# Branch prefetch notes, earlier flag reads and per-pair sink values in a fused attention and mixture-of-experts kernel

## The chip, the cores and the metric

The kernel runs on one core of a Trainium2 chip. The metric is the device time of one execution in microseconds; the time of before is the median of three runs. TensorE (PE, with its weight loads as PEld) multiplies, VectorE (DVE) and ScalarE (ACT) work on its results, GpSimd (POOL) does some elementwise work and the indirect DMAs, and SyncE (SP) issues the other DMAs. Each engine has a sequencer that runs its own program in order: it issues instructions to the engine, waits for semaphores, reads registers from memory and branches.

## The reference

Three stages follow each other, all in float32:

```python
scores = scale * np.matmul(q, k.transpose(0, 1, 3, 2))     # 2 batches, 8 heads, 768 positions, head size 64
keep = is_sink | in_window                                 # first 4 keys, and a window of 128
a = softmax(np.where(keep, scores, -1e9));  attn = a @ v   # reshaped to x: 1536 x 512
for e in range(4):                                         # first mixture: every token, every expert
    out += p[:, e:e + 1] * (np.maximum(x @ w1[e], 0.0) @ w2[e])
idx = argmax(normalised x @ normalised expert_emb / tau)   # second mixture: one of 8 experts per token
out[idx == e] = gate * (np.maximum(x[idx == e] @ w1[e], 0.0) @ w2[e])
```

How many tokens each of the eight experts of the second mixture gets depends on the data.

## The kernel before

Matrix products run as three products of rounded halves (a high part and the remainder), so each float32 operand is first split by a cast (the high part) and a subtraction (the low part).

**Attention** (`Attention.narrow_path`) works on eight pairs of heads. Its instructions are put in order by a small planner (`Order`), which knows for each operation the engine, a planned cost, the operations that it comes after and a rank; it simulates the engines' times and, for each engine, issues among the operations that could start first the one of lowest rank. Loads are operations of SP in this plan. For a query block, scores are made on TensorE (line 365), masked on VectorE (378), put through the exponential on ACT into a probability buffer P (384; two buffers, used by pairs in turn), normalised on POOL (403), transposed on TensorE (410, 412), copied (415) and multiplied with the values (449). The weights of the sink keys are gathered apart and multiplied with the sinks' values in `vsr` (440). `vsr` holds the sinks' values of all eight pairs; it is zeroed at the start by VectorE and POOL and filled by eight DMAs in `vsload` (313). The kernel is written for narrow windows; after attention a flag decides whether a general path recomputes it (`tc.If(att.narrow < 1)`, line 1388). With these inputs it is skipped. `Moe1.first` runs the first hidden layer ahead of that branch, and the first mixture follows it.

**The first mixture** (`moe1`) is a long straight run of matmuls (lines 980 and 1035) with no branch in it.

**The second mixture** (`Moe2.run`) gathers the tokens of an expert in slots of 128 rows. An expert has one slot at least and up to twelve; how many is known only at run time. So each further slot stands in an If inside the one before (`more_slots`): if the flag `over` for slot k + 1 is 0, the program jumps past all the rest of this expert's slots to the next expert. The flag is read from memory into a register of every engine by `Route.has` (line 966, `values_load`); `announced` calls it and marks a branch-hint location. Before, that call names no engines. The bodies are the fall-through side, so the jump is the way out. On the way out each engine runs a few semaphore catch-ups, which wait for its own work so far and raise the counts that the skipped slots would have raised. In the trace they and the branches have line 1297, those of the general path line 1388.

Within a slot (`slot`) the matmuls come in 16 named places: a0 to a3 and b0 to b3 for the first layer, t0 and t1 for transposes of the hidden rows, c0 to c7 for the second layer. Hooks put other engines' work behind these places: the splitting of the next expert's weights (`Fill`, lines 668, 670 and 674) on ACT, VectorE and POOL, with the load of a later chunk behind each, the transposes of the next slot's tokens (1070), and the scaling and scattering of the slot before (1116, 1117). In the first slot of an expert and in the slots inside the Ifs, the flag of the next slot is read ahead of the slot's first matmul:

```python
c = announced(e, 1)
s.gather(xg[1], e, 1)
...
s.paced(e, 0, x0, w, Fill(its, busy), {"c2": [s.split_tokens(xg[1], x1)], ...})
more_slots(e, w, range(1, NT), c)
```

Only expert 0, whose second slot always runs, reads its flag inside a slot, behind place b3.

Of the kernel before, what the change touches and what calls it, by code (L numbers as in the profile page):

```python
# [19 lines left out]
P = 128  # L20
B, H, S, HD = 2, 8, 768, 64
NH = B * H
# [15 lines left out]
SPLIT3 = ((0, 0), (0, 1), (1, 0))  # L38
RANK = dict(
    sc=-1.86, mask=-1.68, exp=2.32, recip=1.03, norm=5.82, scp=-0.61, spe=2.96, sev=1.51, pt=2.75, ev=6.07, av=6.4, avs=4.76, xhi=11.43,  # L40
    xlo=1.57, qpe=-6.05, qhi=-8.82, qlo=-11.56, kpe=-4.73, khi=-2.69, klo=1.91, qld=-11.4, kld=-11.4, vld=-7.72, wld=0, Lpt=5.73, Lsc=-2.22,
    Lav=8.22, Lexp=-2.63, Lnorm=3.72, Lkpe=-4.67, Lavs=11.14, Lrecip=2.17, Lxlo=5.65, Lkhi=-5.14, Lxhi=9.92, Lev=6.37, Lscp=-0.42,
    Lsev=1.82,
)
SLACK = dict(PE=0.02, ACT=0.17, DVE=0.06, POOL=0, SP=0)
GROUP = ((0, 1), (1, 2), (2, 3), (3, 4), (4, 5), (5, 6))
LASTG = ((0, 2), (2, 4), (4, 6))
IOTA = dict(allow_small_or_imprecise_dtypes=True)


# [153 lines left out]
class Attention:  # L204


    def __init__(s, tc, st, c0, ps, q, k, v, n_sink, window, x, ident):

        s.tc, s.nc = tc, tc.nc
        s.q, s.k, s.v, s.x, s.ident = q, k, v, x, ident  # L210
        nc = s.nc
        c1 = st.enter_context(tc.tile_pool(name="a1", bufs=1))
        s.qk = [[c1.tile([P, 6, 2, HD], F32, name=f"{n}r{i}") for i in range(2)] for n in "qk"]
        s.vt = [c1.tile([P, 6, 2, HD], F32, name=f"vt{n}") for n in range(3)]
        s.qs = [c1.tile([P, 2, S], F32R, name=f"qs{n}") for n in range(2)]
        s.kk = [c1.tile([P, 2, 2, KW // 2], F32R, name=f"kk{n}") for n in range(2)]
        s.ksr = c1.tile([NS, NH, HD], F32, name="ksr")
        s.vsr = c1.tile([P, NH // 2, 4, P], F32, name="vsr")
        s.pp = ps.tile([P, 2, 512], F32, name="prep")
        s.xo = [ps.tile([P, 512], F32, name=f"xo{a}") for a in range(2)]  # L220
        V, A, G = nc.vector, nc.scalar, nc.gpsimd
        s.dum = c1.tile([P, P], BF16, name="dum")
        V.memset(s.dum, 0.0)
        s.busy(s.xo[1], 26)
        words = c0.tile([P, 2, 2], I32, name="words")
        h0, h1 = slice(0, 3), slice(3, 6)
        s.load(0, 0, h0)
        s.load(0, 1, h0)
        for i, src in enumerate((n_sink, window)):
            nc.sync.dma_start(out=words[:, i], in_=src.bitcast(I32).partition_broadcast(P))  # L230
        nc.sync.dma_start(out=s.ksr, in_=k[:, :, 0:NS, :].rearrange("b h s d -> s (b h) d"))
        s.load(0, 0, h1)
        s.load(0, 1, h1)
        s.load(1, 0)
        s.load(1, 1)
        s.vload(0)
        e = c1.tile([1, 1], F32, name="warm")
        V.memset(e, 0.0)
        A.activation(e, e, AF.Exp)
        s.rel = c1.tile([P, 2 * P], F32, name="rel")  # L240
        s.key = c1.tile([P, P], F32, name="key")
        G.iota(s.rel, pattern=[[-1, 2 * P]], base=P, channel_multiplier=1, **IOTA)
        G.iota(s.key, pattern=[[1, P]], base=0, channel_multiplier=0, **IOTA)
        G.affine_select(
            out=s.rel, in_=s.rel, pattern=[[-1, 2 * P]], compare_op=ALU.is_ge, fill=3.0e38, base=P, channel_multiplier=1
        )
        s.sk = [c1.tile([P, 4, 32], F32, name=f"sk{n}") for n in range(2)]
        s.masks = c1.tile([P, 4, W], F32, name="masks")
        for t in s.sk:
            G.memset(t, 0.0)  # L250
        V.memset(s.vsr[:, :4], 0.0)
        G.memset(s.vsr[:, 4:], 0.0)
        G.memset(s.masks[:, 0, P:], -1.0e30)
        G.memset(s.masks[:, 1, 2 * P :], -1.0e30)
        s.q_pe(0, s.pp[:, 0], 0)
        s.busy(s.xo[1], 6)
        s.k_pe(0, s.xo[0], 0)
        s.busy(s.xo[1], 18)
        s.q_hi(0, s.pp[:, 0], 0)
        s.k_hi(0, s.xo[0], 0)  # L260
        s.q_lo(0, s.pp[:, 0], 0)
        nw = int64_as_float(nc, c0, words, 2)
        s.nsf, s.wf = nsf, wf = nw[:, 0:1], nw[:, 1:2]
        fl = c1.tile([1, 2], F32, name="fl")
        fi = c1.tile([1, 1], I32, name="fi")
        V.tensor_scalar(fl[:, 0:1], nsf[0:1], float(NS), None, ALU.is_le)
        V.tensor_scalar(fl[:, 1:2], wf[0:1], -1.0, 128.0, ALU.mult, ALU.add)
        V.scalar_tensor_tensor(fl[:, 1:2], wf[0:1], -1.0, fl[:, 1:2], ALU.add, ALU.mult)
        V.scalar_tensor_tensor(fi, fl[:, 1:2], 0.0, fl[:, 0:1], ALU.is_ge, ALU.mult)
        s.k_lo(0, s.xo[0], 0)  # L270
        s.make_masks(c1)
        s.vsload()
        s.narrow = nc.values_load(fi[0:1, 0:1], min_val=0, max_val=1)

    def busy(s, t, n):
# [29 lines left out]
        for x in range(2):  # L305
            s.nc.sync.dma_start(out=s.vt[g % 3][:, :, x, :], in_=s.v[b, h0 + x].rearrange("(c p) d -> p c d", p=P))

    def vsload(s):

        for r in range(4):  # L310
            for x in range(2):
                o = 32 * r + NS * x
                s.nc.sync.dma_start(
                    out=s.vsr[o : o + NS, :, r, x * HD : (x + 1) * HD], in_=s.v[:, x::2, 0:NS, :].rearrange("b h s d -> s (b h) d")
                )

    def q_pe(s, g, pp, a):
        for c in range(3):
# [25 lines left out]
    def narrow_path(s, ctx, late, parts):  # L344
# [5 lines left out]
        masks, sk = s.masks, s.sk  # L350
        skT = [c1.tile([P, P], F32, name=f"skT{n}") for n in range(2)]
        V, A, G = nc.vector, nc.scalar, nc.gpsimd
        hp_ = ctx.enter_context(tc.tile_pool(name="ahd", bufs=2))
        sm = ctx.enter_context(tc.tile_pool(name="asm", bufs=4))
        ps1 = ctx.enter_context(tc.tile_pool(name="aps1", bufs=2, space=PSUM))
        xh, xl = s.x[:, 0], s.x[:, 1]
# [80 lines left out]
        def av_sink(g, i):  # L437
            o = (i % 3) * P
            xo = pr[g]["xo"]
            nc.tensor.matmul(xo[i // 3][:, o : o + P], vsr[:, g, i - 2], skT[g % 2], start=False, stop=True, skip_group_check=True)  # L440

        def av(g, c):
            px, xo = pr[g]["ptx", c], pr[g]["xo"]
# [34 lines left out]
        def all_(name, g, i=range(6), par=(0,)):  # L478
            return [(name, g, x, y) for x in i for y in par]
# [3 lines left out]
        for g in range(NP):  # L483
            groups = LASTG if g == NP - 1 else GROUP
            add("qld", g, 0, 0, dict(SP=2.2 if g else 0.0), lambda e, g=g: g > 1 and s.load(g, 0), [("qpe", g - 2, 0, 0)])
            add("kld", g, 0, 0, dict(SP=2.2 if g else 1.0), lambda e, g=g: g > 1 and s.load(g, 1), [("kpe", g - 2, 0, 0)])
            add("vld", g, 0, 0, dict(SP=2.2 if g else 5.0), lambda e, g=g: g and s.vload(g), all_("av", g - 3) + ([] if g else [("kld", 1, 0, 0)]))
            old = all_("sc", g - 2, par=AB)
            if not g:
                add("qpe", 0, 0, 0, dict(PE=0.32), lambda e: s.q_pe(0, pp[:, 1], 1), [("qld", 0, 0, 0)])  # L490
# [43 lines left out]
                    old.append(("klo", g, 0, 0) if g == NP - 1 else ("xlo", g - 1, c // 2, 0))  # L534
                add("av", *k, dict(PE=0.47 if c < 5 else 0.24), lambda e, g=g, c=c: av(g, c), old)
            for i in range(2, 6):
                add("avs", g, i, 0, dict(PE=0.215), lambda e, g=g, i=i: av_sink(g, i), [("sev", g, 0, 0), ("av", g, i, 0)])
            for a in AB:
                old = all_("avs", g, range(3, 6) if a else [2]) + [("av", g, 3 * a + 2, 0)]
                add("xhi", g, a, 0, dict(ACT=0.37), lambda e, g=g, a=a: x_hi(g, a), old)  # L540
# [561 lines left out]
class Moe2:  # L1102
# [159 lines left out]
    def run(s, psT, sp, wts, hx, wAB):  # L1262
# [26 lines left out]
        def announced(e, k):  # L1289

            c = R.has(e, k)
            tc.mark_branch_hint_location(f"more{e}_{k}", c)
            return c

        def more_slots(e, w, ks, first):

            with ExitStack() as nest:  # L1297
                c = first
                for k in ks:
                    nest.enter_context(tc.If(c > 0, label=f"more{e}_{k}", preferred_fallthrough_block=True))  # L1300
                    more = {}
                    if k < ks[-1]:
                        c = announced(e, k + 1)
                        s.gather(xg[1], e, k + 1)
                        more["c2"] = [s.split_tokens(xg[1], x1)]
                    s.paced(e, k, x1, w, Fill([], busy), more)

        for e in range(E2):
# [3 lines left out]
            if e == 0:  # L1312
                s.gather(xg[0], 1, 0)
                s.gather(xg[1], 0, 2)
                g = s.late
                n = []
                s.second(
                    w,
                    s.x1,
                    Fill(its, busy),  # L1320
                    {
                        "start": g[1:2],
                        "a1": g[2:3],
                        "a3": g[3:4],
                        "b3": g[4:5] + [lambda: n.append(announced(0, 2))],
                        "c2": g[5:] + [s.split_tokens(xg[0], x0)],
                        "c4": [s.split_tokens(xg[1], x1)],
                    },
                )
                more_slots(0, w, range(2, NT), n[0])  # L1330
            else:
                c = announced(e, 1)
                s.gather(xg[1], e, 1)
                if nxt:
                    s.gather(xg[0], e + 1, 0)
                s.paced(e, 0, x0, w, Fill(its, busy), {"c2": [s.split_tokens(xg[1], x1)], "c4": [s.split_tokens(xg[0], x0)] if nxt else []})
                more_slots(e, w, range(1, NT), c)
        s.flush()

    def split_tokens(s, t, o):  # L1340
# [6 lines left out]
def fused(tc, q, k, v, n_sink, window, probs, w1, w2, emb, tau, w1b, w2b, out):  # L1347
# [6 lines left out]
    with st:  # L1354
# [12 lines left out]
        with ExitStack() as sG:  # L1367
# [15 lines left out]
            hx = pool(st, "hx", 2, reuse_waits="tile")  # L1383
            psa = pool(st, "psa", 2, space=PSUM, reuse_waits="tile")
            m1 = Moe1(nc, wts, x, wA, hp, hx, psa)
            tc.mark_branch_hint_location("general", "LikelyTaken")
            m1.first()
            with tc.If(att.narrow < 1, label="general", preferred_fallthrough_block=True):  # L1388
                with ExitStack() as sN:
# [76 lines left out]
```

## Time and profile before

| | us |
|---|---|
| runs: lowest, median, highest of 3 | 914.21, 915.52, 917.66 |
| profiled execution | 916.67 |
| its span, first to last instruction | 914.9 |
| TensorE busy | 875.0 (96%) |
| VectorE busy | 426.8 (47%) |
| ScalarE busy | 303.7 (33%) |
| GpSimd busy | 189.7 (21%) |

The span is the time between the first and the last instruction on the core; the execution's time has a little around it. A timeline row gives start, length, engine, line, operation, tile, shape and how many instructions were merged; brackets at its end give the idle time of the engine before it and what ended that. A q behind an engine (PEq) is its sequencer. Matmul ends are modelled. Reads of registers, branches and semaphore instructions are not counted as busy; the views by line list them with their own lengths, as shortest/median/longest in nanoseconds and the first and last start.

### The profile page before, as it was taken

What the parts mean: (1) busy time and instruction counts of PE and PEld (TensorE: products, weight loads), DVE (VectorE), ACT (ScalarE), POOL (GpSimd) and SP (SyncE); (2) the same over time, 40 slices, a digit from 0 to 9 for tenths busy, and PEclk for the clock granted to TensorE, in tenths of its full rate; (3) what the DMA queues carried; (4) which work ended last, traced back from release to release, by engine and by line L of the source; (5) the groups of instructions that cost most, each with busy time, mean ns of one, the idle gap of its engine ahead of it and who ended that gap; (6) DMA issues with size and microseconds to landing.
All of it is one profiled execution on the core that took longest, in us unless ns stands there. A gap on an engine that the chain in (4) does not pass through costs nothing. (4 is left out here: it accounts for less than half of the span.)

```text
span 914.9 us, 11858 instructions
## 1 busy us (share of the span) xinstructions
PE 875.0 (96%) x4274; PEld 684.3 (75%) x4274; DVE 426.8 (47%) x1013; ACT 303.7 (33%) x664; POOL 189.7 (21%) x284
## 2 busy tenths in 40 slices
PE   8999998999999999999999999999998898898997
PEld 6766666878888888888888888888886676676775
DVE  5786854121234121233121235868547959717611
ACT  4777852020303010302010312111334646525422
POOL 4576510010000000000000000030405737516411
PEclk9999999999999999999999999999999999999999
DMA  7566200030032000023000013000445858727100
GB/s 137 92 144 149 66 24 5 1 116 1 0 93 91 3 0 1 1 92 92 1 1 1 4 66 104 35 12 34 130 154 172 260 156 276 256 74 220 63 34 23
DMA packets 84147, 72.83 MB, mean 80 GB/s; under 512 B 43572, under 2 KB 68148, under 8 KB 84040
## 3 DMA queue, kind: packets, MB, share of 16 engines
q1 hardware_dynamic: 81000, 65.25, 25.0%
q0 software_dynamic: 3040, 6.30, 2.0%
q8 instruction: 49, 0.80, 0.4%
q14 instruction: 58, 0.48, 0.2%
HBM read 68.10 MB, written 7.09 MB: 82 GB/s over the span
## 5 line engine op out<-in xcount | busy, mean ns | idle before, releaser
L1035 PE MATMUL po<-wA,h 128*128 128x512 f32 x1152 | 275.1, 398 | 4.0 <-DVEq L1388 4.0
L980 PE MATMUL ph<-x,wA 128*128 128x512 f32 x1152 | 271.8, 395 | 0.0
L1035 PEld LDWEIGHTS po<-wA,h 128*128 128x128 f32 x1152 | 216.1, 189 | 56.4 <-ACTq L1388 4.4
L980 PEld LDWEIGHTS ph<-x,wA 128*128 128x128 f32 x1152 | 215.2, 187 | 52.7
L982 ACT ACTIVATE h<-ph 128x512 fp32r<-128x512 f32 x96 | 57.4, 597 | 392.4 <-PE ph L980 390.7
L983 DVE SCALAR_TENSOR_TENSOR h<-ph,h 128x512 fp32r<-128x512 f32 x96 | 66.4, 692 | 173.0 <-ACT h L982 173.0
L57 POOL TENSOR_TENSOR gn<-gn,rss 128x4 f32<-128x4 f32 x9 | 1.8, 198 | 443.3 <-DVE gn L55 442.8
L674 DVE TENSOR_TENSOR wA<-raw,wA 128x512 fp32r<-128x512 f32 x107 | 81.3, 789 | 7.2 <-ACT wA L668 5.7
L1045 DVE SCALAR_TENSOR_TENSOR acc<-po,pr,acc 128x512 f32<-128x512 f32 x36 | 27.0, 750 | 110.0 <-PE po L1035 110.0
L668 ACT CAST wA<-raw 128x512 fp32r<-128x512 f32 x115 | 65.9, 618 | 6.4 <-PEq L1297 5.7
L403 POOL TENSOR_TENSOR P<-P,r 128x264 f32<-128x264 f32 (+1 forms) x87 | 54.1, 647 | 48.8 <-DVE r L397 19.5
L1172 PE MATMUL po<-wA,ht 128*128 128x512 f32 x216 | 57.7, 404 | 2.4 <-DVE ht L1166 2.3
L1166 DVE TENSOR_TENSOR ht<-hT,ht 128x512 fp32r<-128x512 f32 x30 | 20.6, 688 | 66.7 <-ACT ht L1165 63.8
L384 ACT ACTIVATE P<-m,nm 128x264 f32<-128x264 f32 x96 | 49.0, 512 | 8.3 <-DVE nm L378 7.9
L1149 PE MATMUL ph<-wA,xt 128*128 128x512 f32 x168 | 43.7, 410 | 7.4 <-PEq L966 7.4
L1172 PEld LDWEIGHTS po<-wA,ht 128*128 128x128 f32 x216 | 38.9, 188 | 11.4 <-DVE ht L1166 3.6
L378 DVE CUSTOM_DVE_ANT_0 m<-sc,masks 128x264 f32<-128x264 f32 x96 | 38.8, 429 | 16.6 <-PE sc L365 15.0
L1149 PEld LDWEIGHTS ph<-wA,xt 128*128 128x128 f32 x168 | 31.9, 194 | 15.7 <-ACTq L1297 6.9
L1149 PE MATMUL ph<-wB,xt 128*128 128x512 f32 x144 | 36.3, 401 | 7.1 <-PEq L966 7.1
L1172 PE MATMUL po<-wB,ht 128*128 128x512 f32 x144 | 39.3, 407 | 3.5 <-DVE ht L1166 3.5
L365 PE MATMUL sc<-kk,qs 64*128 64x264 f32 x288 | 41.6, 339 | 0.7 <-DVE nm L378 0.5
L674 DVE TENSOR_TENSOR wB<-raw,wB 128x512 fp32r<-128x512 f32 x44 | 37.5, 882 | 6.3 <-ACT wB L668 6.1
(222 smaller groups left out, 868.2 us busy)
## 6 DMA issues: line engine op xcount, KB each, us to landing
raw<-in_moe_w_dram SPq DMA_DIRECT2D x96, 512.0 KB
vt<-in_v_dram SPq DMA_DIRECT2D x16, 192.0 KB
xs<-acc SPq DMA_DIRECT2D x12, 256.0 KB
qr<-in_q_dram SPq DMA_DIRECT2D x14, 192.0 KB
kr<-in_k_dram SPq DMA_DIRECT2D x14, 192.0 KB
raw<-en SPq DMA_DIRECT2D x4, 512.0 KB
qr<-in_q_dram SPq DMA_DIRECT2D x4, 96.0 KB
kr<-in_k_dram SPq DMA_DIRECT2D x4, 96.0 KB
```

What stands on the lines that cost most here:

```text
L365: nc.tensor.matmul(sc[:, :W], qs[z, x, i * P : (i + 1) * P], kk[z, y, START[i] : START[i] + W], start=(n == 0), stop=(n == 2))
L378: V.tensor_tensor_reduce(m, t["sc", par][:, :W], masks[:, VAR[i]], -1.0, 3.0e38, ALU.add, ALU.min, t["nm"][:, par, i : i + 1])
L384: A.activation(t["P"][:, par, i], t["m", par, i], AF.Exp, scale=-1.0, bias=t["nm"][:, par, i : i + 1], accum_out=t["su"][:, par, i : i + 1],)
L403: eng.tensor_tensor(y, y, t["r", a][:, par].unsqueeze(2).to_broadcast([P, b - a, W]), ALU.mult)
L668: eng.copy(dst()[:, 0], r)
L674: eng.tensor_tensor(d[:, 1], r, d[:, 0], ALU.subtract)
L980: nc.tensor.matmul(ph, s.wA.w1(a, k, f * P)[:, :P], s.x[:, b, k, tb * TB : (tb + 1) * TB], start=(n == 0), stop=(n == 11))
L982: nc.scalar.activation(t[:, 0], ph, AF.Relu)
L983: nc.vector.scalar_tensor_tensor(t[:, 1], ph, 0.0, t[:, 0], ALU.max, ALU.subtract)
L1035: nc.tensor.matmul(po, hs[f][:, a, t * P : (t + 1) * P], wA.w2(b, f), start=(n == 0), stop=(n == 23))
L1149: nc.tensor.matmul(ph[b], x[:, a, kk], w.w1(c, kk, b * 512), start=(kk == 0 and n == 0), stop=(kk == 3 and n == 2),)
L1172: nc.tensor.matmul(s.po[0], ht[b][:, a, c * P : (c + 1) * P], w.w2(d, f), start=(f == 0 and n == 0), stop=(f == 7 and n == 2),)
```

## The change

Four edits:

- The two calls that mark branch hints name all five engines (`HINTED`), so that each gets a prefetch note: for the general path a fixed one (likely taken), for a slot's flag one that goes by the register.
- The flag of the next slot is read behind place a2 of a slot, and not ahead of its first matmul. The gathers that came behind the read now come ahead of it.
- `vsr` is two buffers of one pair each, used in turn. `vsload(g)` loads one pair by eight DMAs; pair 0's come at the start, the others are an operation `vsl` of SP in the plan, with a rank and a planned cost of 0.8, after the sink matmuls of two pairs before. A pair's sink matmuls come after it. POOL zeroes both buffers.
- P has three buffers. The planner's rule for the exponentials stays as it was.

```diff
+    ... vld=-7.72, vsl=-4, wld=0, ...
+ET = mybir.EngineType
+HINTED = (ET.PE, ET.Activation, ET.DVE, ET.Pool, ET.SP)
...
-        s.vsr = c1.tile([P, NH // 2, 4, P], F32, name="vsr")
+        s.vsr = [c1.tile([P, 4, P], F32, name=f"vsr{n}") for n in range(2)]
...
-        V.memset(s.vsr[:, :4], 0.0)
-        G.memset(s.vsr[:, 4:], 0.0)
+        for t in s.vsr:
+            G.memset(t, 0.0)
...
-    def vsload(s):
-
+    def vsload(s, g):
+
+        b, h0 = divmod(g * 2, H)
         for r in range(4):
             for x in range(2):
                 o = 32 * r + NS * x
-                s.nc.sync.dma_start(
-                    out=s.vsr[o : o + NS, :, r, x * HD : (x + 1) * HD], in_=s.v[:, x::2, 0:NS, :].rearrange("b h s d -> s (b h) d")
-                )
+                s.nc.sync.dma_start(out=s.vsr[g % 2][o : o + NS, r, x * HD : (x + 1) * HD], in_=s.v[b, h0 + x, 0:NS])
...
-        hp_ = ctx.enter_context(tc.tile_pool(name="ahd", bufs=2))
+        hp_ = ctx.enter_context(tc.tile_pool(name="ahd", bufs=3))
...
+            if g:
+                add("vsl", g, 0, 0, dict(SP=0.8), lambda e, g=g: s.vsload(g), all_("avs", g - 2, range(2, 6)))
...
-                add("avs", ..., [("sev", g, 0, 0), ("av", g, i, 0)])
+                add("avs", ..., [("sev", g, 0, 0), ("av", g, i, 0), ("vsl", g, 0, 0)])
...
-            tc.mark_branch_hint_location(f"more{e}_{k}", c)
+            tc.mark_branch_hint_location(f"more{e}_{k}", c, engines=HINTED)
...
                     if k < ks[-1]:
-                        c = announced(e, k + 1)
+                        more["a2"] = [lambda: c.append(announced(e, k + 1))]
                         s.gather(xg[1], e, k + 1)
...
-                c = announced(e, 1)
+                n = []
                 s.gather(xg[1], e, 1)
...
-                s.paced(e, 0, x0, w, Fill(its, busy), {"c2": ...})
-                more_slots(e, w, range(1, NT), c)
+                s.paced(e, 0, x0, w, Fill(its, busy), {"a2": [lambda: n.append(announced(e, 1))], "c2": ...})
+                more_slots(e, w, range(1, NT), n[0])
...
-            tc.mark_branch_hint_location("general", "LikelyTaken")
+            tc.mark_branch_hint_location("general", "LikelyTaken", engines=HINTED)
```

## Rows read from the trace of the kernel before

**Rows 1.** The page's busy times: engine, us, share of the span, instructions.
```profile
PE 875.0 (96%) x4274; PEld 684.3 (75%) x4274; DVE 426.8 (47%) x1013; ACT 303.7 (33%) x664; POOL 189.7 (21%) x284
```
**Rows 2.** Stages: us, length; busy PE, PEld, DVE, ACT, POOL; clock, DMA share, GB/s.
```profile
28.00:124.00 96.00, 95.42 (x751) 65.56 (x747) 74.82 (x292) 75.11 (x223) 57.64 (x101) 1.00 0.44 96
124.00:156.00 32.00, 27.48 (x138) 21.35 (x136) 14.66 (x25) 13.03 (x25) 0.00 (x0) 1.00 0.06 19
156.00:681.00 525.00, 524.82 (x2302) 421.16 (x2303) 184.94 (x410) 93.49 (x176) 22.50 (x61) 1.00 0.14 44
716.00:909.00 193.00, 172.68 (x804) 133.87 (x804) 109.59 (x163) 88.97 (x163) 80.20 (x62) 0.99 0.47 152
```
**Rows 3.** TensorE's waits, whole span: us in total, times, longest.
```profile
PE ph L1149 <- PEq L966: 14.5, 7, 3.1
PE po L1172 <- DVE ht L1166: 5.8, 7, 1.2
PE po L1035 <- DVEq L1388: 4.0, 1, 4.0
```
**Rows 4.** Timeline of TensorE and its weight loads in the second mixture.
```profile
758.53 2.35 PE L1172 MATMUL po<-wA,ht 128*128 128x512 f32 x9
...
762.81 3.32 PEld L1149 LDWEIGHTS ph<-wB,xt 128*128 128x128 f32 x15 [2.38 <-issue]
...
780.68 5.28 PE L1149 MATMUL ph<-wA,xt 128*128 128x512 f32 x15 [3.08 <-PEq L966]
...
809.08 3.67 PE L1149 MATMUL ph<-wA,xt 128*128 128x512 f32 x15
```
**Rows 5.** TensorE's sequencer on lines 1297 and 966: all, and around 760 us.
```profile
L1297 PEldq COMPARE_BRANCH  x18: 65/193/5233, 711.6 to 909.0; - x18
...
L1297 PEldq EVENT_SEMAPHORE  x2: 51/51/51, 762.2 to 762.3; - x2
L1297 PEldq COMPARE_BRANCH  x1: 4119/4119/4119, 758.0 to 758.0; - x1
...
L966 PEldq TENSOR_LOAD <-tr x14: 299/302/322, 707.6 to 892.6; - x14
```
**Rows 6.** The join of the general path: sequencers of line 1388, and timeline.
```profile
L1388 PEldq EVENT_SEMAPHORE  x1: 51/51/51, 152.0 to 152.0; - x1
...
L1388 DVEq EVENT_SEMAPHORE  x1: 21/21/21, 155.8 to 155.8; - x1
...
152.58 0.69 DVE L983 SCALAR_TENSOR_TENSOR h<-ph,h 128x512 fp32r<-128x512 f32 x1 [2.10 <-ACT h L982]
...
155.93 1.40 PE L1035 MATMUL po<-wA,h 128*128 128x512 f32 x5 [4.01 <-DVEq L1388]
```
**Rows 7.** As rows 2, two microseconds behind one change of expert.
```profile
782.00:784.00 2.00, 2.00 (x6) 1.61 (x5) 2.00 (x2) 0.00 (x0) 1.97 (x2) 0.50 0.89 299
```
**Rows 8.** Timeline: VectorE around that change; TensorE and ACT at the end.
```profile
778.75 1.88 DVE L674 TENSOR_TENSOR wA<-raw,wA 128x512 fp32r<-128x512 f32 x3
...
782.49 1.96 DVE L670 CAST wB<-raw 128x512 fp32r<-128x512 f32 x1
...
904.59 3.74 PE L1172 MATMUL po<-wB,ht 128*128 128x512 f32 x15
...
908.86 0.69 ACT L1116 ACTIVATE os<-po,curg 128x512 f32<-128x512 f32 x1 [3.35 <-PEq L1297]
```
**Rows 9.** Attention: the sinks' DMAs on SP, and waits of SP, ACT, PEld.
```profile
L313 SPq DMA_DIRECT2D vsr<-in_v_dram x8: 272/302/964, 11.1 to 15.2; - x8
...
SPq L306 <- PE xo L449: 50.8, 5, 14.5
...
ACT P L384 <- DVE nm L378: 7.9, 22, 0.8
...
PEld pt L410 <- issue: 5.3, 17, 0.4
```
**Rows 10.** Queue of TensorE's instructions, 156 to 681 us: packets, MB, share.
```profile
q8 instruction: 18, 0.29, 0.2%
```

More of the change, by code (lines that the diff above doesn't have):

```diff
@@ L40 @@
     sc=-1.86, mask=-1.68, exp=2.32, recip=1.03, norm=5.82, scp=-0.61, spe=2.96, sev=1.51, pt=2.75, ev=6.07, av=6.4, avs=4.76, xhi=11.43,
-    xlo=1.57, qpe=-6.05, qhi=-8.82, qlo=-11.56, kpe=-4.73, khi=-2.69, klo=1.91, qld=-11.4, kld=-11.4, vld=-7.72, wld=0, Lpt=5.73, Lsc=-2.22,
+    xlo=1.57, qpe=-6.05, qhi=-8.82, qlo=-11.56, kpe=-4.73, khi=-2.69, klo=1.91, qld=-11.4, kld=-11.4, vld=-7.72, vsl=-4, wld=0, Lpt=5.73, Lsc=-2.22,
     Lav=8.22, Lexp=-2.63, Lnorm=3.72, Lkpe=-4.67, Lavs=11.14, Lrecip=2.17, Lxlo=5.65, Lkhi=-5.14, Lxhi=9.92, Lev=6.37, Lscp=-0.42,
@@ L271, in __init__ @@
         s.make_masks(c1)
-        s.vsload()
+        s.vsload(0)
         s.narrow = nc.values_load(fi[0:1, 0:1], min_val=0, max_val=1)
@@ L439, in av_sink @@
             xo = pr[g]["xo"]
-            nc.tensor.matmul(xo[i // 3][:, o : o + P], vsr[:, g, i - 2], skT[g % 2], start=False, stop=True, skip_group_check=True)
+            nc.tensor.matmul(xo[i // 3][:, o : o + P], vsr[g % 2][:, i - 2], skT[g % 2], start=False, stop=True, skip_group_check=True)
         def av(g, c):
@@ L536, in narrow_path @@
             for i in range(2, 6):
-                add("avs", g, i, 0, dict(PE=0.215), lambda e, g=g, i=i: av_sink(g, i), [("sev", g, 0, 0), ("av", g, i, 0)])
+                add("avs", g, i, 0, dict(PE=0.215), lambda e, g=g, i=i: av_sink(g, i), [("sev", g, 0, 0), ("av", g, i, 0), ("vsl", g, 0, 0)])
             for a in AB:
@@ L1297, in more_slots @@
             with ExitStack() as nest:
-                c = first
+                c = [first]
                 for k in ks:
-                    nest.enter_context(tc.If(c > 0, label=f"more{e}_{k}", preferred_fallthrough_block=True))
+                    nest.enter_context(tc.If(c[-1] > 0, label=f"more{e}_{k}", preferred_fallthrough_block=True))
                     more = {}
                     if k < ks[-1]:
-                        c = announced(e, k + 1)
+                        more["a2"] = [lambda: c.append(announced(e, k + 1))]
                         s.gather(xg[1], e, k + 1)
@@ L1335, in run @@
                     s.gather(xg[0], e + 1, 0)
-                s.paced(e, 0, x0, w, Fill(its, busy), {"c2": [s.split_tokens(xg[1], x1)], "c4": [s.split_tokens(xg[0], x0)] if nxt else []})
-                more_slots(e, w, range(1, NT), c)
+                s.paced(e, 0, x0, w, Fill(its, busy), {"a2": [lambda: n.append(announced(e, 1))], "c2": [s.split_tokens(xg[1], x1)], "c4": [s.split_tokens(xg[0], x0)] if nxt else []})
+                more_slots(e, w, range(1, NT), n[0])
         s.flush()
```

## The prediction

> **What bounds the kernel now.** I read the page's head first: TensorE is busy for 875.0 us, 96% of the span [rows 1]. The profiled execution took 916.67 us (914.9 of span and 1.8 around it), 1.15 us above the median of the three runs, 915.52. So only TensorE's idle time, or work added to it, can move the end. The table by stage says where it idles [rows 2]: 0.6 us of 96 in the body of attention, 4.5 us around the join of the general path (124 to 156 us), nothing in the first mixture, and 20.3 us of 193 in the routed experts after 716 us. The list of TensorE's waits names the causes [rows 3]: 14.5 us in seven waits put down to line 966, the read of a slot flag, 5.8 us for VectorE's half of ht, and 4.0 us at the join of line 1388.
>
> The timeline shows that the seven waits stand where one expert hands over to the next, never where a slot is followed by another of its expert: the matmuls of 809.08 carry no gap, while those of 780.68 begin 3.08 us late [rows 4]. A flag is read in both cases, in 302 ns [rows 5], so the read alone is not the stall. The sequencer's instructions of line 1297 tell the rest [rows 5]: of 18 compare-and-branches the shortest took 65 ns, the longest 5233, and the one that jumps at 758.0 took 4119 ns, to 762.12. TensorE's array ran out of matmuls at 760.88 (758.53 + 2.35), with its sequencer still in the branch. Then come two semaphore catch-ups at 762.2 and 762.3, the read, and the first weight load at 762.81 [rows 4, 5].
>
> **The change, part by part.** Durations are of the profiled execution.
>
> *Prefetch notes and early reads at the expert changes.* The calls that mark a branch existed, but named no engines; the trace before has no note among TensorE's sequencer instructions at these branches [rows 5]. Now each of the five engines gets one per flag. If the note does its work, the jump should cost about what a fall-through does, and the sequencer, which reaches the branch some 3 us before the array runs dry (758.0 against 760.88) [rows 4, 5], then waits at the first catch-up until the last matmul retires. At the join such a wait can be seen: TensorE's idling begins at 151.92 (155.93 - 4.01), and its catch-up runs at 152.0 [rows 6], so noticing the array's end costs under 0.1 us. From the branch's end to the first weight load were 0.69 us (762.12 to 762.81), 0.30 of them the read, which is gone from this place: 0.4 us of idling stays. Where more than one slot was run, three changes of the seven, a second, short jump follows, as the 193 ns of the median branch [rows 5]: 0.6 us. So 4 x 0.4 + 3 x 0.6 = 3.4 us stay of 14.5: **11.1 us gained**. The bounds: 2.1 us if only the reads leave (7 x 0.30), 13 us if the catch-ups hide too.
>
> The reads move behind the third group of matmuls, where nine matmuls, 2.1 us, have been issued and cover 0.3 us of reading and one note. The nearest row is a read at a fall-through, behind which the matmuls of 809.08 have no gap [rows 4]. I count it as nothing; uncovered it is 0.30 us for each of 14 flags [rows 5], 4.2 us. SP, POOL, ACT and VectorE issue the same read and note; the first matmul of a slot waits on none of them for it. On POOL the gathers now come before the read.
>
> *A granted clock at 0.50.* [...] With 0.4 us of idling I expect it not to fall: **1.5 us**, between 0 and 1.6, since it followed one change of seven.
>
> *What is late next.* VectorE still splits weights after the slot has ended: its last ones end at 780.63, when TensorE's matmuls had ended at 777.60 (780.68 - 3.08) [rows 4, 8]. Before, the stall hid that. With a start at 778.0, TensorE needs VectorE's half of the first ht behind 24 matmuls, 12 at 809.08's rate to each of two halves, some 6 us later, at 784.0; VectorE has three splits of the next slot ahead of it, of which one took 1.96 us [rows 8] and the others about 0.6 (1.88 for three), 3.2 us, and then 0.6 for ht itself: 784.4. So some 0.4 us is lost at each of two such places, and the 5.8 us [rows 3] stay. I take back **1.0 us**, with bounds of 0 and 4 (0.6 us for each of seven).
>
> *The join of the general path.* TensorE waits 4.0 us for VectorE's catch-up at 155.8; VectorE's last result was there at 153.27 [rows 3, 6]. With the note VectorE catches up at 153.3, and TensorE starts at 153.5: **2.4 us**. TensorE's own jump is over by 152.0, so it is not the term. The note lies 25 us ahead of the branch; if it is lost by then, 0.
>
> *The last exit.* The final scatter's scaling on ACT waits for TensorE's catch-up until 908.86, when the matmuls had ended at 908.33 [rows 8]; 0.2 us of that stays: **0.3 us**.
>
> *Sinks' values.* Seven groups of eight DMAs are added on SP, at 0.30 us each [rows 9] 2.4 us in a pair of some 14 us. SP spends 50.8 us of the attention waiting for TensorE in five waits of line 306 [rows 9], which covers the 17 us, and the loads behind a group are issued a pair ahead of their use. A group waits for the sink matmuls of two pairs before and is needed most of two pairs later, so I expect no wait. But TensorE's sequencer gets about 28 semaphore instructions more, four to a pair, of 51 ns [rows 5], 0.15 us if one stands alone; its weight loads idle for 5.3 us on issue in this stage, so it is not always ahead [rows 9]. Bounds 0 and 4.2 us; I take **1.0 us**, near the 51 ns row. Two long memsets, VectorE's and POOL's, shrink at the start, before anything there waits for them: 0. The planner's order may move a little.
>
> *Third probability buffer.* ACT's exponentials waited in attention for VectorE alone, 7.9 us in 22 waits, never for the readers of the old buffer [rows 9], and the planner's rule for them is unchanged: 0.
>
> **Sum.** 916.67 - 11.1 - 1.5 - 2.4 - 0.3 + 1.0 + 1.0 = 903.4 us against that execution. The median lies 1.15 us lower, part of which may be the half clock, so the forecast for the median is 903.0 us.
>
> **The rivals.**
> *The notes are lost where code moves on.* TensorE's instructions come in pieces of 16 KB (18 packets, 0.29 MB in the first mixture) [rows 10]. If the sequencer holds few pieces, the note's piece is given up when it crosses into the next one before the branch. In the first mixture, which doesn't branch, 18 pieces came in 525 us, one per 29 us [rows 10]; of a slot of 13 us the last 11 lie behind the note, so some 40% of the notes have a crossing behind them: three changes of seven. They keep 2.07 us each (14.5 over 7) less the 0.5 that would stay: 3 x 1.6, with the read gone 4 us: 907 us.
> [...]
>
> *The notes do nothing.* The registers might tell the prefetcher too late, or the landing may not be what the 4 us are. For it: no row shows a note at work. Against: a jump differs from the shortest branch by 4.05 us, far more than a branch needs. Then the reads give 2.1 us and the sinks take 1.0: 914.4 us, no change.
>
> *The notes displace what is needed next.* One mechanism on the other side: a note fetches its target in place of the piece that the slot is about to run, and the sequencer stalls in the slot. Such a fetch costs 4.1 us [rows 5] and early in a slot the sequencer is only about 1 us ahead: 3.1 us for a slot. Of 14 noted slots with 40% crossing a piece, six would pay 18 us while three of seven changes keep their stall: 903 + 4 + 18 = 925 us. With the rest as forecast the change is slower than before from five stalled slots on (12.5 us over 3.1). Against it: where the flag is set the note carries that the branch falls through.
>
> *Sinks dear.* All 28 semaphore instructions uncovered and VectorE's takings at their bound, 4.2 + 4 instead of 2: 909 us.
>
> **How the numbers follow.** Forecast 0.60, notes partly lost 0.14, notes without effect 0.13, displaced code 0.08, sinks dear 0.05. This kernel can tell about 0.5%, 4.6 us, from no change. Faster takes the first, second and fifth, less a few parts for a sum of small losses: 0.75. Same is 0.17, slower 0.08. The forecast's own range is 899 to 907; 8 in 10 need the second and fifth case and some depth below (catch-ups hidden, VectorE's waits shrinking): 898 to 911.
>
> **What would show it.** In the profile after, TensorE's jumps of line 1297 should take under 0.3 us and the note should appear as an instruction of its own; seven waits at the expert changes should sum to about 3.4 us; the clock should stay at 1.00 at 782; the join's wait should be about 1.5 us; the flag reads should begin inside slots with no TensorE wait behind them; attention should end within 1 us of before. It is wrong if jumps still take 4 us, if waits "on issue" appear inside slots, if TensorE's wait for ht grows by more than 4 us, or if attention ends over 4 us later.

## The result, and the profile after

| | us |
|---|---|
| changed kernel, median of 4 runs (lowest, highest) | 903.5 (899.9, 904.9) |
| kernel before, 4 runs beside it | 916.6 (914.2, 918.6) |
| ratio, 95% interval | 0.9852 (0.9812 to 0.9893) |
| profiled execution, its span | 899.87, 898.1 |

The forecast was 903.0. The sum came out right, its parts did not. In the changed kernel the lines from 488 on have moved down by 3, attention's ahead of them by 1 to 3.

TensorE's busy time, answering [rows 1]:

```profile
PE 866.0 (96%) x4274; PEld 678.0 (75%) x4274; DVE 422.4 (47%) x1012; ACT 302.2 (34%) x664; POOL 189.0 (21%) x285
```

The same 4274 matmuls kept it busy 9 us less, so some of them ran faster: idling alone is not the story. The table by stage, columns as in [rows 2]:

```profile
28.00:124.00 96.00, 95.25 (x759) 66.06 (x756) 72.42 (x275) 72.44 (x214) 53.89 (x94) 1.00 0.46 101
124.00:156.00 32.00, 30.38 (x131) 24.19 (x130) 13.15 (x24) 9.90 (x18) 0.00 (x0) 1.00 0.06 19
156.00:681.00 525.00, 524.11 (x2324) 421.05 (x2323) 192.67 (x437) 99.85 (x189) 23.78 (x63) 1.00 0.14 46
716.00:898.00 182.00, 163.12 (x767) 126.20 (x765) 98.79 (x150) 83.24 (x152) 75.52 (x58) 0.99 0.46 147
```

Around the join TensorE is 2.9 us busier in the same 32 us. In the first mixture nothing idles, as before; the 0.9 us of the third row, where 0.2 were, lie in the routing, of which the same window now holds more. The last rows can't be compared as they stand, since the work comes over 10 us earlier and the window after holds 6.1 us behind the last matmul: from 716 us to the last matmul 12.8 us are idle (to 891.90), where 19.7 were (to 908.33).

TensorE's waits over the whole span, answering [rows 3]:

```profile
PE po L1175 <- DVE ht L1169: 5.0, 6, 1.0
PE ph L1152 <- PEq L1300: 4.6, 5, 2.5
PE ph L1152 <- ACTq L1300: 3.5, 2, 2.7
PE hT L1166 <- ACT hh L1160: 2.0, 1, 2.0
...
PE po L1038 <- DVEq L1391: 1.6, 1, 1.6
```

The wait for the read is gone from the list, but 4.6 + 3.5 us stand at the same places under other names. TensorE's sequencer, answering [rows 5]: notes, reads, all branches of line 1300, then one at a time those that leave experts 2, 3 and 5.

```profile
L1455 PEldq BRANCH_PREFETCH_HINT  x15: 30/35/52, 0.8 to 877.5; - x15
...
L969 PEldq TENSOR_LOAD <-tr x14: 300/306/317, 695.7 to 877.1; - x14
...
L1300 PEldq COMPARE_BRANCH  x18: 65/200/5036, 701.4 to 892.2; - x18
...
L1300 PEldq COMPARE_BRANCH  x1: 4854/4854/4854, 747.3 to 747.3; - x1
...
L1300 PEldq COMPARE_BRANCH  x1: 5036/5036/5036, 764.7 to 764.7; - x1
...
L1300 PEldq COMPARE_BRANCH  x1: 346/346/346, 822.0 to 822.0; - x1
```

A note took 35 ns in the median. Where it worked, the jump took 0.33 to 0.37 us instead of 3.5 to 5.2; that holds for experts 1, 4, 5 and 6 and the last exit. The jumps out of experts 0 (3.85), 2 and 3 are as slow as before. The prediction had named jumps that still take 4 us as a sign of being wrong, and three of eight do. The join of the general path, VectorE's catch-up and TensorE's start, answering [rows 6]:

```profile
L1391 DVEq EVENT_SEMAPHORE  x1: 21/21/21, 145.4 to 145.4; - x1
```
```profile
145.60 1.63 PE L1038 MATMUL po<-wA,h 128*128 128x512 f32 x6 [1.62 <-DVEq L1391]
```

And what no row of before had told me to look at: the same six score matmuls near 10.6 us, first before, then after, in TensorE's timeline.

```profile
10.76 1.03 PE L365 MATMUL sc<-kk,qs 64*128 64x264 f32 x6
```
```profile
10.52 0.64 PE L366 MATMUL sc<-kk,qs 64*128 64x264 f32 x6
```

They take 1.03 us up to 27.5 us before, 0.64 from 10.5 us after. In both profiles the clock column shows 1.00 there, but the clock record begins only at 27.5 and 10.5 us; later profiles have the stretch in their record, at 0.50.

Where the 16.8 us between the two spans went, by the ends of TensorE's matmuls: up to the join's idling 7.9 (151.92 against 143.98); the join 2.4 (4.01 against 1.62 of idling); from there to the routing's first transpose 1.6 (504.4 against 502.8); from there to the last matmul 4.6 (248.03 against 243.47); behind it 0.4. So the second mixture brought far less than forecast, and the start, where I expected a small loss, most.

### The profile page after: what moved, and what is told of

Same layout as the page of the kernel before. It is cut to its first block, busy times and chain, and to the rows that moved or that the text cites. A ratio compares the mean times of both kernels' runs of the same rounds, so it can differ in the third digit from the quotient of the medians.

```text
span 898.1 us, 12016 instructions
## 1 busy us (share of the span) xinstructions
PE 866.0 (96%) x4274; PEld 678.0 (75%) x4274; DVE 422.4 (47%) x1012; ACT 302.2 (34%) x664; POOL 189.0 (21%) x285
## 5 line engine op out<-in xcount | busy, mean ns | idle before, releaser
L677 DVE TENSOR_TENSOR wB<-raw,wB 128x512 fp32r<-128x512 f32 x44 | 40.1, 938 | 4.2 <-ACT wB L671 3.7
L765 DVE CUSTOM_DVE_ANT_0 rj<-acc,raw 128x512 f32<-128x512 f32 x64 | 40.1, 687 | 0.2
```

The lines of the kernel that those rows point to most:

```text
L677: eng.tensor_tensor(d[:, 1], r, d[:, 0], ALU.subtract)
L765: s.nc.vector.tensor_tensor_reduce(j, s.acc[:, tt], s.eb[e], 1.0, 0.0, ALU.mult, ALU.add, s.dl[:, tt, e : e + 1])
```

## The experiments

Each was timed beside the kernel before, whose median was 916.1 to 916.5 in all three groups; single runs of one kernel spread over 3 to 16 us. Edits are shown as parts of the difference from the changed kernel, with three dots for lines left out. A note or jump is called lost where the jump is as slow as without a note, and caught where it is short.

**Attention edits alone**

```diff
-            tc.mark_branch_hint_location(f"more{e}_{k}", c, engines=HINTED)
+            tc.mark_branch_hint_location(f"more{e}_{k}", c)
...
-                        more["a2"] = [lambda: c.append(announced(e, k + 1))]
+                        c = announced(e, k + 1)
```

> The kernel before with the attention edits alone (sinks' values by pairs, three probability buffers, POOL's two small memsets); no notes, flags read where they were. Theory A, from the two profiles: the attention edits bring the 7.9 us by which TensorE's matmuls reach the join earlier (143.98 us against 151.92), most of it before 28 us, where the changed kernel had 179 matmuls done and the kernel before 136. Then this run is 6 to 9 us faster than before, about 908.5, with its join gap (4.0 us) and its seven jumps of 3.5 to 5.2 us as before. Rival B, my forecast: the edits cost about 1 us, 917.5, and the early 7.9 us are chance: the start of an execution, where matmuls take 1.6 times as long up to some moment (10.5 us in one profile, 27.4 in the other), ends at a different moment in each execution. Then this run is within 1.5 us of before in the median, and its profile shows a slow stretch of some other length.

917.06 us, ratio 1.0004 (0.9974 to 1.0034). Theory A fell: the early 7.9 us are not the edits' (some 2 of them are, as the traces show below). This profile's start, and its stretch behind the join (columns as in [rows 2]; the granted clock is the third number from the end):

```profile
9.00:26.00 17.00, 16.19 (x76) 11.78 (x73) 10.06 (x43) 10.40 (x33) 7.26 (x18) 0.50 0.83 136
...
152.00:160.00 8.00, 6.80 (x17) 5.36 (x18) 0.88 (x5) 0.00 (x0) 0.00 (x0) 0.57 0.02 4
```

The slow start is TensorE at a granted clock of 0.50. Over the 14 profiles it lasted until 10.5 or 27.5 us from the outset (3 profiles), or came back some 8 us in for 3.4 to 20.5 us (8), or neither (3, two of them the runs below in which the first gap is filled). Old attention had 10 to 27 us of it, new attention 0 to 27. In this run the record shows it again behind the join for 6.8 us, and for 20.5 us in five stretches from the routing on.

At full clock the edits do show. From the 800th matmul ahead of the join to the last one, three profiles with the old attention took 112.94 to 112.95 us, eleven with the new one 110.73 to 110.80: 2.2 us less, where I had charged 1.0. The same comes out from the 700th; shorter counts do not measure it (1.4 us less from the 600th, 0.7 more from the 500th), because the planner orders the work otherwise and they begin in other work. Which of the two edits does it was not tried.

**Notes and reads alone**

```diff
-        s.vsr = [c1.tile([P, 4, P], F32, name=f"vsr{n}") for n in range(2)]
+        s.vsr = c1.tile([P, NH // 2, 4, P], F32, name="vsr")
...
-        hp_ = ctx.enter_context(tc.tile_pool(name="ahd", bufs=3))
+        hp_ = ctx.enter_context(tc.tile_pool(name="ahd", bufs=2))
```

> The kernel before with the notes on all engines and the reads inside the slots; attention as before. Theory A: 2.4 us at the join and about 4.5 us in the second mixture, 909.5 us, 7 us faster than before; three of seven jumps still cost 3.8 to 5.0 us, though not the same three need be lost, as TensorE's code stands some twenty instructions elsewhere. Rival B: nearly the whole gain of the changed kernel is here, 904 us.

908.14 us, 0.9898 (0.9865 to 0.9931), near theory A. On TensorE the notes of experts 2 and 3 were lost (jumps of 5.07 and 5.63 us); expert 0's worked (0.45).

**Notes on TensorE alone**

```diff
-HINTED = (ET.PE, ET.Activation, ET.DVE, ET.Pool, ET.SP)
+HINTED = (ET.PE,)
```

> The changed kernel with the notes on TensorE alone. In both profiles no other engine has a jump over 0.3 us, so I expect the time of the changed kernel within 1 us, 903.5, and the same three jumps (of experts 0, 2 and 3) at 3.8 to 5.0 us, since TensorE's program is the same: what decides whether a note works would then be the place in the code. Rival: chance in the moment decides, and other jumps are lost. Rival on the join: VectorE needs its own note there, and the gap at the join is back at 4.0 us (906).

910.04 us, 0.9924 (0.9891 to 0.9958): the rival on the join held. VectorE and TensorE there, with what ended the idle time before them:

```profile
153.81 0.06 DVE L734 MEMSET rcum<- 128x4 uint32 x1 [2.52 <-DVEq L1391]
```
```profile
153.64 1.62 PE L1038 MATMUL po<-wA,h 128*128 128x512 f32 x3 [3.77 <-DVEq L1391]
```

TensorE's own jump took 0.40 us, and still it waited 3.77. My reading that no other engine has slow jumps was wrong: at the join VectorE's branch record is short (72 ns) and the stall stands behind it, up to the next record of its sequencer, 2.9 us later; ACT's is like it (50 ns, 2.5 us). So here VectorE needs its own note. TensorE's program is that of the changed kernel, and experts 2 and 3 were lost again (5.15, 4.50), expert 0 not (0.45).

**Reads alone, with the attention edits**

```diff
-            tc.mark_branch_hint_location("general", "LikelyTaken", engines=HINTED)
+            tc.mark_branch_hint_location("general", "LikelyTaken")
...
-            tc.mark_branch_hint_location(f"more{e}_{k}", c, engines=HINTED)
+            tc.mark_branch_hint_location(f"more{e}_{k}", c)
```

> The changed kernel without any note: reads inside the slots and the attention edits stay. By the prediction's rows a read leaves each of seven changes, 7 x 0.30 = 2.1 us less than the attention edits alone; TensorE's eight jumps take 3.5 to 5.2 us again and the join 4.0. So the changed kernel plus 2.4 (join) plus the four jumps that its notes had caught, 4 x 1.8: some 912. Rival: reads inside the slot bring nothing, since the sequencer is ahead by more than a read: 914.

916.60 us, 1.0002 (0.9967 to 1.0038). Of the two expectations 912 lies outside this interval and the rival's 914 inside. Yet the trace shows the reads gone from the changes: TensorE's idling there is 12.0 us, against 14.5 before and 15.2 in the run with the attention edits alone (both runs' sums with one wait of 1.7 to 2.0 us on issue just behind a change). The 2.1 us of the reads are there, but too little for the time to show.

**The changed kernel again** (no edit; its marks, as they were)

```diff
             tc.mark_branch_hint_location(f"more{e}_{k}", c, engines=HINTED)
```

> The changed kernel itself once more, beside the others. Theory A: its first ratio, 0.985, was helped by executions with a short slow stretch at the start (10.5 us in its profile), which the edits don't decide; then it comes to what the notes with the reads brought alone, 0.990, some 908, and its profile may show a start of either length. Rival B: edits act together, and 0.985 stands, 903. In its profile the jumps of experts 2 and 3 take 4.5 to 5.6 us, as in all three kernels with notes so far, and the others under 0.5.

902.66 us, 0.9848 (0.9815 to 0.9881). Theory A fell; the first ratio was no luck. Lost again: experts 2 and 3 (3.60, 4.74), but not 0 (0.45).

**The note behind b3**

```diff
-                        more["a2"] = [lambda: c.append(announced(e, k + 1))]
+                        more["b3"] = [lambda: c.append(announced(e, k + 1))]
```

> The changed kernel with read and note behind place b3 instead of a2: some sixty of TensorE's instructions after a slot's start instead of twenty, and about 5 us ahead of the jump, where expert 0's note already stands. Theory A: a note that comes within some 4 us of a landing from a jump can be lost (experts 2 and 3: 1.2 to 4.3 us after it), since the next piece of code is then on its way; behind b3 all eight jumps take under 0.5 us and the two gaps of 2.5 to 3.1 us shrink to 0.6: 4 us less than the changed kernel. Rival B: what decides lies in the place of these experts' code, not in the note's: experts 2 and 3 stay at 4.5 to 5.6 us, and the time is unchanged. Rival C: 5 us is too short, as for expert 0 in one profile of two; then three or more jumps are slow and the time is 2 to 6 us longer.

903.34 us, 0.9837 (0.9803 to 0.9871): no difference. TensorE's jumps out of experts 0, 2 and 3:

```profile
L1300 PEldq COMPARE_BRANCH  x1: 3827/3827/3827, 706.3 to 706.3; - x1
...
L1300 PEldq COMPARE_BRANCH  x1: 4570/4570/4570, 751.0 to 751.0; - x1
...
L1300 PEldq COMPARE_BRANCH  x1: 3920/3920/3920, 769.6 to 769.6; - x1
```

Theory A fell: some 4 us more between the landing and the note don't help experts 2 and 3.

**The note given twice**

```diff
                         more["a2"] = [lambda: c.append(announced(e, k + 1))]
+                        more["b3"] = [lambda: c.append(announced(e, k + 1))]
```

> The changed kernel with read and note at a2 and again behind b3. Theory A: whichever of the two is taken serves, all eight jumps under 0.5 us, 4 us less than the changed kernel; the 14 additional reads and notes of 0.35 us are hidden. Rival B: a second note for the same branch starts nothing, and experts 2 and 3 stay slow.

901.32 us, 0.9828 (0.9794 to 0.9863). All TensorE's branches, then TensorE and ACT at the change behind expert 3:

```profile
L1300 PEldq COMPARE_BRANCH  x18: 65/198/458, 705.2 to 892.8; - x18
```
```profile
770.57 1.66 PE L1152 MATMUL ph<-wA,xt 128*128 128x512 f32 x6 [2.42 <-ACTq L1300]
```
```profile
770.74 1.14 ACT L671 CAST wB<-raw 128x512 fp32r<-128x512 f32 x2 [3.03 <-ACTq L1300]
```

Every jump of TensorE is caught, as theory A has it, but 1.3 us were gained and not 4, and that is within the intervals. At the changes TensorE now idles 6.9 us, against 8.3 and 8.1 in the changed kernel: behind expert 3 ACT is late. It had done its last cast at 767.71 and runs its catch-up at 770.50; why is not shown.

That the second note is what caught the two jumps is not shown either. The notes and reads added in experts 0 and 1 move the code of experts 2 and 3 by some 40 instructions (an estimate from the kernel's loops, 20 notes with a read each), and the next run, and one with 36 instructions more, catch both with one note.

**The code moved**

```diff
+        for _ in range(extra):
+            nc.tensor.matmul(ph, s.wA.w1(0, 0, f * P)[:, :P], s.x[:, 0, 0, tb * TB : (tb + 1) * TB], start=True, stop=True)
...
-            s.hidden(0, f, s.hs[f])
+            s.hidden(0, f, s.hs[f], 8)
```

The last line is in `again`, which only the general path calls.

> The changed kernel with 64 more matmuls in the general path, which is never run, so that TensorE's later code stands 128 instructions, half a piece of 16 KB, further on; nothing that runs is changed. If the place of a note in its piece decides, experts 2 and 3 are no longer the lost ones, and others may be; if the moment decides (so many us after a landing, or the loads then under way), experts 2 and 3 still take 4.5 to 5.6 us.

A single run, 902.88 us. The jumps out of experts 2 and 3:

```profile
L1302 PEldq COMPARE_BRANCH  x1: 350/350/350, 751.8 to 751.8; - x1
...
L1302 PEldq COMPARE_BRANCH  x1: 328/328/328, 769.3 to 769.3; - x1
```

From 156 to 681 us of before, where 18 pieces came for 2302 matmuls and 2303 weight loads [rows 2, 10], a piece holds about 256 of TensorE's instructions, and 128 are half of one (an estimate). Nothing that runs was changed, and the two notes lost in five profiles of five now work. So for these two it matters where the code lies. Which property of the place it is stays open: it isn't the note's own offset in a piece by itself, since with a2 and b3, some forty instructions apart, the same two were lost.

**Notes and reads, once more** (the edit of the second run)

```diff
-        s.vsr = [c1.tile([P, 4, P], F32, name=f"vsr{n}") for n in range(2)]
+        s.vsr = c1.tile([P, NH // 2, 4, P], F32, name="vsr")
```

> The kernel of the run with notes and reads and the old attention once more. Its ratio was 0.990, that of the changed kernel twice 0.985, and the attention edits alone 1.000: these don't add up by some 5 us. Theory A: chance in the starts (a stretch at half clock of 0 to 20 us after TensorE's first gap), then 0.985 to 0.988 here, 903 to 906. Rival B: the attention edits are worth 5 us once the notes are there, then 0.990 again, 908.

907.15 us, 0.9899 (0.9864 to 0.9933), rival B's number. Attention alone brings nothing, the notes alone 1.0%, both 1.5%. Each interval is 0.3 to 0.4% to either side, so the 0.5% that don't add up may be chance, though the notes alone and both together each came out the same twice. The traces give the attention edits 2.1 us (matmuls end at 151.99 here and at 149.87 in the run with notes on TensorE alone, with the same 20.5 us of half clock at the start), and the stretch from the routing on took 244.9 and 244.1 us in the two profiles with old attention, 243.5 and 242.6 in those of the changed kernel; the rest isn't settled.

**The first gap filled**

```diff
+        if g == 0 and a == 0:
+            s.busy(s.xo[1], 18)
         o = 256 if a else 384
         nc.tensor.transpose(pp[:, o : o + NS], s.ksr[:, 2 * g : 2 * g + 2].rearrange("p h d -> p (h d)"), s.ident[:NS, :NS])
```

> The changed kernel with 18 more of its small warm-up matmuls (0.107 us each, results not used) ahead of the first transpose of the sinks' keys, where TensorE idles for 1.6 to 2.4 us at 6 us, waiting for their load. In every profile whose clock record covers it the granted clock falls to 0.50 some 0.3 to 1.5 us after that gap ends. Theory A: the gap is what lets it fall; filled, the first 28 us stay at 1.00, and 3 to 10 us are gained over the changed kernel, about 898 in the median. Rival B: the fall belongs to the time since the start, or to the gaps of 0.5 us behind it, and comes all the same: the time of the changed kernel, 903. TensorE's later code stands 36 instructions further on, so other notes may be lost than in experts 2 and 3: plus or minus 5 us.

899.82 us (five runs from 899.1 to 900.2, one at 907.3), 0.9845 (0.9798 to 0.9892). TensorE at that place in its timeline, and the first 28 us by stage; then, for comparison, the gap unfilled in the run of the moved code that follows, and its 9 to 26 us:

```profile
7.79 0.22 PE L338 MATMUL xo<-ident,ksr 8*128 8x8 f32 x1 [0.98 <-DMA ksr<-in_k_dram]
```
```profile
0.00:28.00 28.00, 24.52 (x207) 19.33 (x207) 18.32 (x83) 19.41 (x59) 15.31 (x43) 1.00 0.71 126
```
```profile
7.70 0.22 PE L336 MATMUL xo<-ident,ksr 8*128 8x8 f32 x1 [1.95 <-DMA ksr<-in_k_dram]
```
```profile
9.00:26.00 17.00, 16.32 (x75) 11.84 (x73) 9.87 (x44) 10.65 (x34) 7.56 (x19) 0.51 0.82 134
```

The gap shrank to 0.98 us and the clock didn't fall. By 28 us 207 matmuls were done, 18 of them the added ones; the other 189 are as many as in the changed kernel's second profile, whose clock didn't fall either with a gap of 1.69 us. So the expectation's "every profile" was wrong: of nine profiles with the gap unfilled and its end in the record eight fell, two of them just before that end. The median is 3 us below the changed kernel's, but the ratio is the same; that it is faster is not shown. With the code 36 instructions further on, experts 2 and 3 were caught (0.43 both), and 0 and 5 lost (3.89, 4.93).

**The moved code, timed** (the edit of the moved code above)

```diff
+            s.hidden(0, f, s.hs[f], 8)
```

> The changed kernel with the later code 128 instructions further on, timed. In its one look the jumps of experts 2 and 3 took 0.35 and 0.33 us, the last one 1.12. Two gaps of 2.2 to 2.7 us at the expert changes are gone or shorter: 2 to 4 us less than the changed kernel, 899 to 901, unless VectorE's and ScalarE's work of the slot is then what TensorE waits for (902).

902.92 us, 0.9862 (0.9818 to 0.9906). The expected 2 to 4 us did not come. Experts 2 and 3 were caught (0.35, 0.34), expert 0 was lost this time (3.65), and behind expert 2 TensorE waited 2.14 us all the same, for ACT.

**Both**

```diff
+        if g == 0 and a == 0:
+            s.busy(s.xo[1], 18)
...
+                        more["b3"] = [lambda: c.append(announced(e, k + 1))]
```

> The changed kernel with the first gap filled and the note given twice. Theory A: both gains add, 3 to 10 us from the start and about 1.5 us from the second notes (901.3 against 902.7): 895. Rival B, as for the filled gap alone: 901.

900.25 us (897.5 to 901.5), 0.9833 (0.9793 to 0.9873). No half clock in the first 28 us again, and no jump over 0.86 us. Two to three microseconds below the changed kernel in the median, not separated from it by the intervals; 895 was not reached.

## Why the time was right and the sum was not

**Expert changes, 11.1 us forecast: about 6.3.** TensorE's idling there went from 14.5 to 8.3 and 8.1 us in the two profiles of the changed kernel, not to 3.4. The failing step is "if the note does its work": it did at four and five of the seven changes. At experts 1, 4, 5 and 6, where it did, 0.3 to 0.6 us stayed, as worked out (0.4 and 0.6); at experts 2 and 3 it was 2.2 to 2.7. Expert 0's note made no difference there: 0.73 us stayed with it lost and 1.15 with it caught, both times put down to ACT.

So the first rival happened, with its count of three in the first profile and its size (2.07 each) at two of them. Its mechanism, "given up when it crosses into the next one", is not what lost most of them. The queue of TensorE's instructions, between expert 0's note and its jump, lists two other queues and no q8 in the first profile of the changed kernel, where the jump was lost (696.2 to 701.4 us), and one piece in the second, where it was caught (695.4 to 700.4):

```profile
q1 hardware_dynamic: 1063, 1.06, 68.8%
q0 software_dynamic: 4, 0.00, 0.2%
```
```profile
q8 instruction: 1, 0.02, 1.3%
```

In the eleven profiles with notes each of the 70 caught jumps has exactly one piece of 16 KB between its (first) note and the jump; of the 18 lost ones 14 have none, and the other four, all expert 3's, one that came 0.5 to 1.9 us behind the note. So at 14 of 18 nothing was fetched that could be given up. In the first profile of the changed kernel the jump out of expert 5, with its piece there, took 0.35 us, and that out of expert 2, with none, 4.85. Why no piece came stays open.

**The join, 2.4 us forecast: right**, with its cause: VectorE catches up when its last result is there (at 145.4, the result at 145.39), and without VectorE's own note TensorE waits 3.77 us with its own jump at 0.40.

**ACT, not in the sum.** At the changes I looked at TensorE's jump alone. ACT is the limit at two of them: 3.5 us in two waits after, 3.9 with every TensorE jump caught. The trace of before had it already, at the two longest of the seven waits (3.08 us behind expert 3, 2.96 behind 5). Behind expert 3 ACT ends its last casts at 777.16 and runs its catch-up at 780.1:

```profile
776.02 1.14 ACT L668 CAST wA<-raw 128x512 fp32r<-128x512 f32 x2
```
```profile
L1297 ACTq EVENT_SEMAPHORE  x2: 17/17/17, 780.1 to 780.2; - x2
```

Every later profile has one such hole of 2.2 to 3.5 us behind expert 2, 3 or 5, with notes on ACT and without. So no run shows that ACT's own notes do anything at the changes.

**Reads, 2.1 us of the 11.1: about right**, 2.5 us in the trace of the run without notes, and no wait put down to any of the 14 reads in the slots.

**The granted clock, 1.5 us forecast: more, and in other places.** I priced one fall that one profile showed: after 3.08 us of idling, fifteen matmuls in 5.28 us instead of 3.67 [rows 4], at a granted clock of 0.50 [rows 7]. Over all profiles, falls to 0.50 lasted 3.4 or 6.8 us behind a gap, and up to 20.5 us at the start. Behind the join one came in four profiles of four with a gap of 3.8 to 4.1 us and in none of ten with 1.6; the stage that follows is then 1.6 to 2.8 us longer. That was part of the price of the join and I had left it out. From the routing on the three profiles without notes had 3.4, 20.5 and 13.7 us of it, the two of the changed kernel 3.4 each (the other nine with notes 3.4 to 10.2), and the profile I worked from was the lightest of the three: its second mixture, from the routing on, took 248 us, that of the attention run 255, of the reads run 251.

**VectorE late, 1.0 us lost: about right, by another wait.** The waits for ht went from 5.8 to 5.0 instead of up, and one new wait of 2.0 us came, for ACT's hh in the slot behind expert 0's change: 1.2 us lost together, 0.6 in the second profile of the changed kernel.

**Last exit, 0.3: right.** ACT's scaling begins 0.18 us behind the last matmul, 0.53 before.

**Sinks' values, 1.0 us lost, and third buffer, nothing: wrong in sign together.** Attention is 2.1 to 2.2 us shorter at equal clock with the two edits. The bounds, 0 and 4.2, left out a gain and gave no reason for it; which of the two terms was wrong, and what shortens it, stays open.

**The start.** The 7.9 us of the first comparison are some 2.1 us of attention and for the rest the half clock, which ended at 10.5 us in one execution and at 27.5 in the other; the run with attention alone shows no such gain in the median.

So the sum by what was measured: changes 6.3, join 2.4, clock behind it 1.6 to 2.8, attention 2.1, exit 0.3, less 0.6 to 1.2 for the late engines: 11.5 to 13.3, against 13 to 14 us between the medians. What is left may be fewer falls of the clock at the changes and at the start; that is argued from single profiles and not shown. The forecast was right by luck: changes overrated by 5 us were made up by clock and attention underrated by about as much.

## What to carry to other kernels

A stall of TensorE where it sets the time can have two prices: its length, and what the clock takes behind it (at the join here 2.4 us and 1.6 to 2.8); ask for the second wherever a gap of some microseconds goes. Look for an engine's jump not only in its branch record but in the hole up to its sequencer's next one (VectorE's at the join: 72 ns, and 2.9 us behind them), and give notes to every engine that others wait for (there TensorE waited 3.77 us without VectorE's note, 1.62 with it); then look whether each was caught. One profile can't price what differs from execution to execution: before believing an early gain, see the same stage in a second profile of the same kernel.

## What was not expected of the hardware

- Whether a prefetch note works can hang on where the code lies: the same two of eight were lost in six profiles with one note at a2 or b3, and moving the code by 128 instructions without changing what runs mended both, in two profiles of two. Expert 0's note was lost in one execution and not in the other of the same program, in three programs: 3.85 and 0.45 us in the changed kernel, 4.35 and 0.45 with the old attention, 3.65 and 0.45 with the code moved.
- A second note for the same branch did TensorE's jumps no harm: all eight between 0.35 and 0.46 us in one profile, up to 0.86 in the other. On POOL the catch-up behind expert 1 came 4.9 and 5.2 us after its branch in these two, against 0.4 to 0.5 in all others.
- TensorE's granted clock fell to 0.50 for 3.4 to 20.5 us around gaps of only 1.4 to 4.1 us, though not at each: the gaps of 2.2 to 2.7 us behind experts 2 and 3 in the changed kernel brought no fall. A profile may have no clock record for its first 27 us; there the durations of like matmuls (1.03 against 0.64 us) are what tells.
